# Transposes in pairs of 64-row tiles, output blocks split between ScalarE and GpSimd, and a new instruction order in a fused attention and feed-forward kernel

## Chip, cores and metric

The kernel runs on one core of a Trainium2 chip. The metric is the device time of one execution in microseconds, lower is better. Engines are named as in the profile: PE (TensorE), DVE (VectorE), ACT (ScalarE), POOL (GpSimd), SP (SyncE, which only issues DMAs here).

## What is computed

```python
B, N, m, C = (4, 12480, 32, 128)
scale = 1.0 / np.sqrt(C)
I = np.broadcast_to(inducing[None], (B, m, C))
def mab(q, kv):
    s = scale * (q @ kv.transpose(0, 2, 1))
    s = s - s.max(-1, keepdims=True)
    a = np.exp(s)
    a /= a.sum(-1, keepdims=True) + 1e-09
    return a @ kv
h = mab(I, x)                       # 32 inducing points attend to 12480 rows
attn = mab(x, h)                    # 12480 rows attend to the 32 results
# then, row by row, with w_in [128, 2048] and w_out [2048, 128]
hid = attn @ w_in
out = (hid * np.clip(hid + 3.0, 0.0, 6.0) / 6.0) @ w_out
```

The feed-forward is hid * (hid + 3) / 6 as long as hid lies between -3 and 3: a linear part and a part in products of hid with itself. Since each attention row is a weighted mean of only 32 vectors, the kernel works out the feed-forward of those 32 once per batch (the linear part) and of their pairs (the products), and then gives each row a weighted sum of these coefficients. No 2048-wide hidden layer is ever made for the rows.

## The kernel before

**Tiles.** Each batch of 12480 rows is cut into six groups of 2048 rows (16 tiles of 128 rows) and one small group of 192 rows. Everything is indexed by batch b and group g; g = 6 is the small one.

**Order.** The program is one long list, ORDER (lines 20 to 149), of tokens such as `T.1.2.8.16.6`. Each token calls a function `op_<name>` with the numbers as arguments, and each of these issues a few instructions on one engine. Every engine, and each DMA queue, runs its own instructions in the order of the list and waits where a tile that it needs isn't ready. Letters at a token's end (V, A, P) choose DVE, ACT or POOL. The last number or numbers are banks of PSUM; there are eight banks.

**First attention**, per group: X loads x as 16 bit (POOL's queue, seven buffers xh for the whole groups); T transposes it on PE, eight tiles of 128x128 into one bank; Y copies the bank to xT; S multiplies with the inducing points; E takes the exponential (ACT); A sums x with those weights on PE; H adds that to hacc (DVE).

**Coefficients**, per batch, when all H are done: c3 to cB norm the 32 vectors; G multiplies them with w_in in three parts (a high and a low half of w_in, made by wh and wl at the start); cG writes the result to GL; cD makes two 16-bit copies in Gd. The linear part: cH adds 3 and clips at 0 into r6 (POOL, line 543), cI clips at 6 and multiplies by GL (DVE, line 548), L multiplies with w_out, and cL, cM, cm, cN carry it on. The products: p makes four tiles PR of products of pairs (line 609, 128x2048 each), P multiplies them with w_out on PE (line 616, wb makes the 16-bit w_out), and cP, cX, cY write the result to Cq. cJ takes the largest magnitude of GL for a test at the end; cQ and cC do likewise for other bounds.

**Second attention and output**, per group: Z makes the scores on PE (32-column tiles), Zd, Zz and Ze scale and exponentiate them, W copies some of them to more partitions by DMA (SP's queue, line 698), ee squares (line 692), B spreads the scores on PE in tiles of 32 rows (line 731), F takes the exponential from PSUM to TF (ACT, line 741), U multiplies TF with d into TD (DVE, line 750). Then l (line 770, pairs of 64-row tiles) and q (line 789) build output blocks of 128x512 in a bank: four blocks a group, each of one l and four q for the two factors TF and TD. R, Rr and R2 make the scale r of each row; v multiplies a block by r into os: DVE in one instruction (line 807), ACT in four of 128x128 (line 811). O writes a group's os to DRAM (SP's queue). There are two buffers os, so a group's v wait for the O of two groups earlier.

**Ahead and behind.** w are warming matmuls on zeros. i0 to i9 make constants. y0 to y5 count, at the very end, whether all bounds hold; if one doesn't, the kernel runs `direct_path`, a slow plain version.

Of the kernel before, what the change touches and what calls it, by code (L numbers as in the profile page):

```python
# [9 lines left out]
FP32 = mybir.dt.float32  # L10
# [15 lines left out]
T.0.4.8.16.4 Y.0.4.8.16.4.V S.0.2.0.16.5 E.0.2.0.16.5 H.0.0.0.8.6 X.0.6.0.2 A.0.3.0.16.2 wh.0.A wl.0.V A.0.2.0.16.5
S.0.4.8.16.6 S.0.4.0.8.1 wi.1 T.0.5.8.16.4 T.0.6.0.2.3 T.0.5.0.8.0 E.0.4.0.8.1 Y.0.6.0.2.3.V S.0.6.0.2.7 Y.0.5.0.8.0.V
A.0.4.0.8.3 H.0.3.0.16.2 H.0.4.0.8.3 Y.0.5.8.16.4.A X.1.1.0.16 S.0.5.8.16.4 wh.2.V E.0.6.0.2.7 S.0.5.0.8.1 wh.3.V
E.0.5.8.16.4 X.1.0.0.16 wo.1 A.0.6.0.2.0 H.0.6.0.2.0 A.0.5.8.16.4 wo.0 E.0.4.8.16.6 A.0.4.8.16.7 H.0.5.8.16.4
E.0.5.0.8.1 H.0.4.8.16.7 H.0.2.0.16.5 A.0.5.0.8.6 H.0.5.0.8.6 c3.0.0 wl.3.V T.1.1.0.8.5 c7.0.V wl.1.P c8.0.V  # L30
T.1.1.8.16.4 i7.P G.0.1.2 wl.2.P G.0.3.2 G.0.2.2 Y.1.1.8.16.4.A c4.0.0 c9.0 cB.0.P G.0.0.2 cK.0 Z.0.2.1.7 Zd.0.2.7 cA.0
Z.0.0.0.1 Y.1.1.0.8.5.V cG.0.2 Z.0.0.1.5 Zd.0.0.5 W.0.0.0 W.0.0.2 Z.0.1.1.3 Zz.0.0.1 Z.0.1.0.2 Zd.0.1.3 Zz.0.1.2 W.0.0.1
cD.0.0.V T.1.0.8.16.0 T.1.0.0.8.4 X.1.3.0.16 cH.0.P cD.0.1.A Y.1.0.8.16.0.V S.1.1.0.16.6 Y.1.0.0.8.4.A W.0.0.3
E.1.1.0.16.6 Z.0.3.0.5 Z.0.2.0.7 cI.0 Zz.0.2.7 p.0.2.V W.0.2.3 B.0.0.0.2.0 S.1.0.0.16.4 F.0.0.0.0.2 E.1.0.0.16.4 L.0.0.6
A.1.1.0.16.7 W.0.2.0 H.1.1.0.16.7 L.0.1.6 cL.0.6 p.0.1.V A.1.0.0.16.4 cM.0.0.6 W.0.1.0 Ze.0.0 cm.0.3 ee.0.0.V cN.0.3
# [120 lines left out]
TG = 16  # L156
# [27 lines left out]
def kernel(  # L184
# [35 lines left out]
    with ExitStack() as es:  # L220
# [78 lines left out]
        def veng(e):  # L299
            return {"V": nc.vector, "P": nc.gpsimd}[e]  # L300
# [241 lines left out]
        def op_cH(b, e):  # L542
            veng(e).tensor_scalar(
                r6[:, :, :], GL[:, :, :M].bitcast(FP32), 3.0, 0.0, op0=ALU.add, op1=ALU.max
            )
# [485 lines left out]
```

## Time and profile before

| what | us |
|---|---|
| median of 3 runs | 248.84 |
| lowest and highest run | 248.77 and 250.02 |
| the profiled execution | 249.51 |
| its span, first to last instruction | 247.5 |

The profile describes one execution. Busy time of an engine is the time in which one of its instructions ran; matmuls overlap in their pipeline, so PE's busy time is not its peak rate. A row of the timeline has the start, the time from first start to last end, engine, line, operation, output and inputs, and how many instructions were merged; in brackets the idle time of the engine ahead of it and what ended it. A row of a group has busy time, mean ns of one, and the idle time ahead of them with its releasers. A row of waits has the total, how often, and the longest.

### The profile page before, as it was taken

To read this page: it belongs to the slowest core of one execution; us is meant where nothing else is said; L and a number is where in the kernel's file an instruction comes from. 1 tells how busy PE (TensorE), PEld (TensorE's weight loads), DVE (VectorE), ACT (ScalarE), POOL (GpSimd) and SP (SyncE) were. 2 spreads that over 40 slices of the span, in tenths; PEclk is the share of its full clock that TensorE was granted. 3 is DMA by queue.
4 is the path that set the end of the run, shared out by engine and by line. 5 is a ranking of instruction groups with operands and counts; after the bars stand their busy time and mean duration, and the time that the engine had idled before them with its cause. 6 is when DMAs were issued, how large, how long until landed. Compare 5 with 4: busy or idle time off the path is not lost. (4 is left out here: it accounts for less than half of the span.)

```text
span 247.5 us, 10076 instructions
## 1 busy us (share of the span) xinstructions
PE 227.0 (92%) x4317; PEld 186.5 (75%) x4317; DVE 202.4 (82%) x438; ACT 191.1 (77%) x350; POOL 40.3 (16%) x80
## 2 busy tenths in 40 slices
PE   1879799999799999999899999999999999989990
PEld 0568758888698798797787888888878877768780
DVE  0236879989599997999778998988889999998983
ACT  2167277998788886999687786999889889989870
POOL 8518582021002500010004000000031000000000
PEclk9999679999999999999999999999999999999998
DMA  6999789969989999849879974623981849696953
GB/s 96 193 255 254 238 158 193 208 163 250 214 286 263 277 196 331 293 87 250 184 252 265 266 274 110 224 56 76 338 305 37 262 97 340 211 311 170 362 232 134
DMA packets 23744, 53.91 MB, mean 218 GB/s; under 512 B 3697, under 2 KB 16785, under 8 KB 20753
## 3 DMA queue, kind: packets, MB, share of 16 engines
q1 hardware_dynamic: 19072, 38.36, 47.4%
q0 software_dynamic: 4624, 14.88, 31.0%
q8 instruction: 34, 0.56, 0.8%
q14 instruction: 14, 0.11, 0.1%
HBM read 27.67 MB, written 25.56 MB: 215 GB/s over the span
## 5 line engine op out<-in xcount | busy, mean ns | idle before, releaser
L741 ACT ACTIVATE TF<-ps 128x1024 f16<-128x1024 f32 (+1 forms) x100 | 96.8, 1007 | 16.1 <-PE ps L731 12.4
L750 DVE TENSOR_TENSOR TD<-TF,d 128x2048 f16<-128x2048 f16 (+1 forms) x52 | 59.9, 1156 | 3.0 <-ACT TF L741 2.2
L789 PE MATMUL ps<-Cq,TF 128*128 128x128 f16 (+1 forms) x784 | 57.9, 219 | 2.6 <-issue 1.4
L789 PE MATMUL ps<-Cq,TD 128*128 128x128 f16 (+1 forms) x784 | 56.0, 219 | 0.0
L807 DVE TENSOR_TENSOR os<-ps,r 128x512 f32<-128x512 f32 x68 | 45.4, 683 | 11.7 <-PE ps L789 4.1
L789 PEld LDWEIGHTS <-TF 128*128 128x128 f16 (+1 forms) x784 | 46.3, 98 | 6.3 <-issue 6.0
L789 PEld LDWEIGHTS <-TD 128*128 128x128 f16 (+1 forms) x784 | 46.1, 99 | 4.3 <-issue 3.4
L811 ACT ACTIVATE os<-ps,r 128x128 f32<-128x128 f32 x112 | 32.0, 380 | 4.3 <-PE ps L789 2.0
L422 PE MATMUL ps<-ident_h,xh 128*128 128x128 f16 x384 | 29.8, 226 | 5.5 <-DMA xh<-in_x_dram 5.5
L422 PEld LDWEIGHTS <-xh 128*128 128x128 f16 x384 | 24.0, 102 | 11.6 <-DMA xh<-in_x_dram 7.5
L428 DVE COPY xT<-ps 128x1024 f16<-128x1024 f16 x31 | 21.2, 684 | 12.8 <-PE ps L422 12.5
L428 ACT COPY xT<-ps 128x1024 f16<-128x1024 f16 x17 | 17.0, 1015 | 18.9 <-PE ps L422 18.8
L416 POOL DMA_DIRECT2D xh<-in_x_dram x25 | 13.9, 560 | 75.1 <-PE ps L459 62.2
L731 PE MATMUL ps<-z,pair 32*128 32x256 f16 (+1 forms) x400 | 20.3, 270 | 0.0
L609 DVE TENSOR_TENSOR PR<-Gd 128x2048 bf16<-128x2048 bf16 x16 | 19.8, 1239 | 0.0
L678 DVE TENSOR_SCALAR_CACHE_REDUCE z<-ps 128x512 f16<-128x512 f32 (+1 forms) x28 | 17.3, 621 | 2.4 <-PE ps L656 2.3
L666 ACT ACTIVATE dk<-ps 128x512 f16<-128x512 f32 (+1 forms) x28 | 14.8, 547 | 5.5 <-PE ps L656 3.4
L770 PE MATMUL ps<-BD,ee 64*128 64x256 f16 (+1 forms) x196 | 17.5, 273 | 0.2
L441 ACT ACTIVATE a<-ps 128x512 f16<-128x512 f32 (+1 forms) x27 | 14.6, 556 | 2.6 <-PE ps L433 2.6
L616 PE MATMUL ps<-w_ob,PR 128*128 128x128 bf16 x256 | 16.5, 219 | 0.0
L671 ACT ACTIVATE e<-z 128x512 f16<-128x512 f16 (+1 forms) x28 | 16.3, 589 | 0.1
L616 PEld LDWEIGHTS <-PR 128*128 128x128 bf16 x256 | 14.7, 98 | 0.9 <-issue 0.8
(137 smaller groups left out, 284.8 us busy)
## 6 DMA issues: line engine op xcount, KB each, us to landing
out_dram<-os SPq DMA_DIRECT2D x23, 1024.0 KB, 5.2
d<-dk SPq DMA_DIRECT2D x96, 128.0 KB, 3.9
xh<-in_x_dram POOLq DMA_DIRECT2D x23, 512.0 KB, 8.8
os<-in_moe_w_in_dram POOLq DMA_DIRECT2D x2, 512.0 KB, 13.4
w_or<-in_moe_w_out_dram POOLq DMA_DIRECT2D x2, 512.0 KB, 11.6
out_dram<-os SPq DMA_DIRECT2D x2, 512.0 KB, 3.6
xh<-in_x_dram POOLq DMA_DIRECT2D x2, 256.0 KB, 7.3
out_dram<-osl SPq DMA_DIRECT2D x4, 96.0 KB, 3.0
```

Source lines behind the costliest of these rows:

```text
L422: nc.tensor.transpose(pt[:, (i - lo) * p : (i - lo + 1) * p], at(xh, xhl, b, g)[:p, i, :], ident_h[:p, :p])
L428: copier(e)(xT_of(b, g)[:, lo * p : hi * p], ps[:, k, :].bitcast(FP16)[:, : (hi - lo) * p])
L609: veng(e).tensor_mul(pr_of(b, c)[:, :, :].rearrange("p a (i m) -> p a i m", m=M), views[0], views[1])
L616: nc.tensor.matmul(ps[:, k, f * C : (f + 1) * C], lhsT=pr_of(b, c)[:, jb, :], rhs=w_ob[:, jb, :], start=first_of(b, u), stop=False, skip_g ...
L678: nc.vector.tensor_scalar(fat(z_, b, g)[:rows, :w], ps[:rows, k, :w], 1.0, None, op0=ALU.mult, op1=ALU.min, accum_out=z_all[:rows, b * NGR ...
L731: nc.tensor.matmul(ps[:, pairs[j // 2] + j % 2, f * w : (f + 1) * w], lhsT=pair[rows, f, :], rhs=fat(z_, b, g)[rows, h * w : (h + 1) * w], ...
L741: nc.scalar.activation(hat(TF_, b, g, h)[:, 2 * q : 2 * q + 2, :w], ps[:, k : k + 2, :w], ACT.Exp, scale=scale / KH)
L750: nc.vector.tensor_mul(split(hat(TD_, b, g, h)), split(hat(TF_, b, g, h)), d.unsqueeze(2).to_broadcast([P, J, 2, w]),)
L770: nc.tensor.matmul(ps[:p, ks[jp], s2 * 2 * C : (s2 + 1) * 2 * C], lhsT=fat(e2_, b, g)[rows, s * p : (s + 1) * p], rhs=BD_[b % 2][rows, :, ...
L789: nc.tensor.matmul(ps[:p, k, (s2 * 2 + j2) * C : (s2 * 2 + j2 + 1) * C], lhsT=t[:, j, f * w + s2 * p : f * w + (s2 + 1) * p], rhs=Cq_[b % ...
L807: nc.vector.tensor_mul(o, src, r.unsqueeze(3).to_broadcast([p, Sh, 2, C]))
L811: nc.scalar.mul(o[:, s2, j2, :], src[:, s2, j2, :], r[:, s2, j2 : j2 + 1])
```

## The change

Four things change beside the order of the list.

1. Transposes of the whole groups of batches 1 to 3 (18 groups): TT moves a tile of 128 rows as two transposes of 64 rows, one on the upper and one on the lower half of the array, into two banks; one TT is a whole group, 32 matmuls of 64 columns in place of 16 of 128. YY copies each of the two banks to xT with a stride, 128x1024 as Y does. Batch 0 and the small groups keep T and Y.
2. 13 of 100 output blocks are copied unscaled by ACT in one instruction (`v...C`) and then multiplied in place by POOL (`m`). The others: 64 on DVE (70 before) and 23 on ACT with scaling (30 before).
3. The clip is gone: cI multiplies GL + 3 by GL straight from GL, cH and r6 are removed. The test at the end takes the sum of the squares of GL along each partition (ACT) with a bound of 9, in place of the largest magnitude (DVE) with a bound of 3.
4. Engines: 14 of 28 ee and 4 of 16 p run on POOL, some copies swap between DVE and ACT.

In the list, batch 0's loads come ahead of w_in (w_in's first half stood before its last groups), three groups of batch 1 come ahead of w_out, there are 26 warming matmuls in place of 16, and of the last group R, R2 and the counts y0, y1, y2 stand earlier.

```diff
+        def op_TT(b, g, *ks):
+            for i in range(TG):
+                for r in range(2):
+                    rows = slice(64 * r, 64 * r + 64)
+                    nc.tensor.transpose(
+                        ps[:, ks[r], :].bitcast(FP16)[:, i * 64 : (i + 1) * 64],
+                        at(xh, xhl, b, g)[rows, i, :],
+                        ident_h[rows, rows],
+                        tile_position=(64 * r, 0),
+                    )
+
+        def op_YY(b, g, r, k, e):
+            copier(e)(
+                xT_of(b, g)[:, :].rearrange("c (i r t) -> c r i t", r=2, t=64)[:, r],
+                ps[:, k, :].bitcast(FP16).rearrange("c (i t) -> c i t", t=64),
+            )
...
-        def op_cH(b, e):
-            veng(e).tensor_scalar(
-                r6[:, :, :], GL[:, :, :M].bitcast(FP32), 3.0, 0.0, op0=ALU.add, op1=ALU.max
-            )
-
         def op_cI(b):
             nc.vector.scalar_tensor_tensor(
-                GL[:, :, M:], r6[:, :, :], 6.0, GL[:, :, :M].bitcast(FP32), op0=ALU.min, op1=ALU.mult
+                GL[:, :, M:],
+                GL[:, :, :M].bitcast(FP32),
+                3.0,
+                GL[:, :, :M].bitcast(FP32),
+                op0=ALU.add,
+                op1=ALU.mult,
             )
 
         def op_cJ(b):
-            nc.vector.tensor_reduce(
-                g_all[:, b : b + 1],
+            nc.scalar.activation(
+                junk[:, :].rearrange("p (a m) -> p a m", m=M),
                 GL[:, :, :M].bitcast(FP32),
-                axis=AX.XY,
-                op=ALU.max,
-                apply_absolute_value=True,
+                ACT.Square,
+                accum_out=g_all[:, b : b + 1],
             )
...
-            if e == "V":
+            if e == "C":
+                nc.scalar.copy(o, src)
+            elif e == "V":
                 nc.vector.tensor_mul(o, src, r.unsqueeze(3).to_broadcast([p, Sh, 2, C]))
...
+        def op_m(b, g, h, jp):
+            t0, p, J, Sn = groups[g]
+            Sh = (Sn + 1) // 2
+            o = at(os_, osl, b, g)[:p, : J * Sn, :].rearrange("p (s j) c -> p s j c", j=J)
+            o = o[:, h * Sh : (h + 1) * Sh, 2 * jp : 2 * jp + 2, :]
+            r = r2_of(b, g, 0, J * Sn).rearrange("p (s j) -> p s j", j=J)
+            r = r[:, h * Sh : (h + 1) * Sh, 2 * jp : 2 * jp + 2]
+            nc.gpsimd.tensor_mul(o, o, r.unsqueeze(3).to_broadcast([p, Sh, 2, C]))
...
-            count(3, g_all[:, :], 3.0, ALU.is_le)
+            count(3, g_all[:, :], 9.0, ALU.is_le)
```

The new list around the coefficients of batch 0 and the first q, as it stands (TT and YY carry batch, group and banks or half):

```diff
+E.0.4.0.8.6 X.1.3.0.16 X.1.0.0.16 A.0.5.0.8.4 wo.0 A.0.4.0.8.5 w.2.6 wh.3.V wl.3.V E.0.4.8.16.7 wo.1 E.0.5.8.16.0
+A.0.5.8.16.3 wh.0.A H.0.6.0.2.2 X.1.6.0.2 H.0.5.0.8.4 H.0.4.0.8.5 A.0.4.8.16.1 H.0.5.8.16.3 X.1.2.0.16 TT.1.1.3.2
...
+E.1.0.0.16.7 H.1.1.0.16.0 Ze.0.1 wb.1.P Zz.0.0.1 B.0.0.0.4.0 F.0.0.0.0.4 W.0.1.0 Zz.0.2.6 p.0.1.V L.0.1.3 A.1.0.0.16.2
...
+p.0.3.V Z.0.3.0.7 P.0.0.6 R2.0.1.V cP.0.0.6 Zz.0.3.7 X.1.4.0.16 P.0.3.2 TT.1.5.4.0 TT.1.2.7.1 cN.0.3 Ze.0.2 ee.0.2.V
```

More of the change, by code (lines that the diff above doesn't have):

```diff
@@ L26 @@
[L26 to L35, printed above, removed]
@@ L151 @@
[L151 to L152 removed]
+i2 w.2.5 w.2.0 X.0.0.0.16 i1 i8 w.2.2 w.2.0 w.2.4 i0 w.2.5 i4.1 i3.V w.2.4 i5.1.V X.0.6.0.2 T.0.6.0.2.7 Y.0.6.0.2.7.A
+w.2.1 X.0.1.0.16 T.0.0.8.16.4 Y.0.0.8.16.4.V T.0.0.0.8.6 Y.0.0.0.8.6.V X.0.2.0.16 S.0.0.8.16.0 E.0.0.8.16.0 S.0.0.0.8.2
+i6 A.0.0.8.16.5 E.0.0.0.8.2 A.0.0.0.8.3 w.2.7 T.0.1.0.8.2 Y.0.1.0.8.2.V T.0.1.8.16.6 X.0.3.0.16 w.2.4 S.0.6.0.2.1
@@ new lines @@
+l.0.1.1.5.7 ee.0.4.V v.0.1.1.0.5.A ee.0.3.P Z.0.5.1.6 Zd.0.5.6 q.0.2.0.1.1.4 q.0.2.0.1.0.4 B.0.3.0.2.0 F.0.3.0.1.0
+v.0.1.1.1.7.V l.0.2.0.5.4 TT.2.4.6.7 q.0.2.0.0.1.5 S.1.4.0.16.0 F.0.3.0.0.2 X.3.0.0.16 U.0.2.1 E.1.4.0.16.0
+q.0.2.0.0.0.5 R2.0.2.V O.0.0.0.16 v.0.2.0.1.4.C YY.2.4.0.6.V Z.0.5.0.2 m.0.2.0.1 YY.2.4.1.7.V B.0.3.1.6.0 F.0.3.1.0.6
+X.2.3.0.16 q.0.2.1.0.1.3 v.0.2.0.0.5.V W.0.3.2 W.0.3.1 Zz.0.5.2 R.0.4.4 Rr.0.4.4 U.0.3.0 q.0.2.1.1.1.5 F.0.3.1.1.0
+W.0.4.2 q.0.2.1.1.0.5 q.0.2.1.0.0.3 l.0.2.1.3.5 W.0.4.3 B.0.4.0.6.0 v.0.2.1.1.5.V A.1.4.0.16.2 H.1.4.0.16.2
@@ new lines @@
+q.1.3.1.0.0.7 cJ.1 cC.2 Rr.1.6.6 q.1.3.0.0.0.4 v.1.3.0.0.4.V B.1.4.1.0.2 F.1.4.1.1.2 l.1.3.1.7.6 ee.1.6.V G.2.2.5
+G.2.3.5 F.1.4.1.0.0 cG.2.5 cI.2 q.1.3.1.1.0.6 cD.2.1.A q.1.3.1.1.1.6 B.1.5.0.2.4 F.1.5.0.0.2 cA.2 S.3.1.0.16.1 cD.2.0.V
+L.2.0.0 U.1.4.0 q.1.3.1.0.1.7 v.1.3.1.1.6.A W.1.5.2 p.2.2.V q.1.4.1.1.0.3 ee.1.4.P v.1.3.1.0.7.A L.2.1.0 cL.2.0
+E.3.1.0.16.1 q.1.4.1.0.0.6 q.1.4.0.0.0.2 q.1.4.0.0.1.2 U.1.4.1 p.2.3.P l.1.4.1.6.3 l.1.4.0.2.1 W.1.6.0 F.1.5.0.1.4
+TT.3.4.7.0 YY.3.4.0.7.V W.1.5.3 O.1.2.0.16 v.1.4.0.0.2.A TT.3.2.4.5 YY.3.2.1.5.V YY.3.2.0.4.A q.1.4.1.1.1.3
@@ new lines @@
+l.2.0.0.3.1 H.3.3.0.16.7 O.1.4.0.16 v.1.6.0.0.2.V B.2.1.0.4.6 q.2.0.0.0.0.3 Ze.2.3 F.2.1.0.0.4 R.2.2.0 q.2.0.0.0.1.3
+q.2.0.0.1.1.1 ee.2.1.V U.2.0.1 F.2.1.0.1.6 S.3.5.0.16.2 Rr.2.2.0 q.2.0.1.1.0.4 v.2.0.0.0.3.A R2.2.1.V W.2.1.2
+A.3.4.0.16.5 E.3.5.0.16.2 q.2.0.0.1.0.1 W.2.1.1 W.2.1.3 U.2.1.0 H.3.4.0.16.5 v.2.0.0.1.1.V Z.2.4.0.0 Z.2.4.1.5 Zd.2.4.5
+B.2.1.1.6.2 dr Zz.2.4.0 A.3.5.0.16.1 q.2.0.1.1.1.4 H.3.5.0.16.1 F.2.1.1.0.6 W.2.2.3 c3.3.1 R.2.3.0 Rr.2.3.0
+q.2.0.1.0.0.5 c4.3.1 q.2.0.1.0.1.5 F.2.1.1.1.2 U.2.1.1 R2.2.2.V l.2.0.1.5.4 v.2.0.1.0.5.C m.2.0.1.0 B.2.2.0.0.6
@@ L153 @@
+q.3.5.1.0.0.4 Ze.3.6 q.3.5.1.0.1.4 F.3.6.0.0.0 U.3.6.0 v.3.5.0.1.6.A ee.3.6.V v.3.5.0.0.5.V q.3.6.0.0.0.2 v.3.5.1.0.4.V
+R.3.6.1 Rr.3.6.1 R2.3.6.V l.3.6.0.2 m.3.4.1.0 O.1.6.0.2 O.3.4.0.16 O.3.5.0.8 y1 v.3.5.1.1.7.A q.3.6.0.0.1.2 O.3.5.8.16
+y3 y4.3 y5.3 v.3.6.0.0.2.A O.3.6.0.2
 """
@@ L258 @@
         Gd = sb.tile([P, FB, 2 * M], BF16, name="Gd")
-        r6 = sb.tile([P, FB, M], FP32, name="r6")
         LV = sb.tile([2 * M, C], FP32R, name="LV")
```

228 lines of the change are left out of this document (106 added, 122 removed).

## The prediction

> **What bounds the kernel now.** I read the page first (share of each engine, the 40 slices), then the busy time in three stretches, then the waits of the longest stretch.
>
> ```profile
> span 247.5 us, 10076 instructions
> PE 227.0 (92%) x4317; PEld 186.5 (75%) x4317; DVE 202.4 (82%) x438; ACT 191.1 (77%) x350; POOL 40.3 (16%) x80
> PE   1879799999799999999899999999999999989990
> PEclk9999679999999999999999999999999999999998
> DMA  6999789969989999849879974623981849696953
> ```
>
> The reader is to see TensorE near nine tenths in nearly every slice but the first seven and the last, a clock that drops in slices 5 to 7, and DMA engines near full over that same start.
>
> ```profile
> 0.00:47.40 47.40, 37.46 (x690) 29.43 (x691) 27.60 (x66) 25.84 (x40) 24.70 (x58) 0.93 0.93 200
> 47.40:241.00 193.60, 189.17 (x3625) 156.91 (x3623) 172.54 (x352) 164.62 (x309) 15.56 (x22) 1.00 0.77 224
> 241.00:247.50 6.50, 0.39 (x7) 0.14 (x5) 2.29 (x22) 0.62 (x2) 0.00 (x0) 0.84 0.40 149
> 27.00:33.90 6.90, 6.24 (x91) 4.56 (x92) 4.91 (x16) 2.77 (x5) 3.19 (x4) 0.51 0.82 205
> 47.38 1.05 PE L789 MATMUL ps<-Cq,TF 128*128 128x128 f16 x16
> ACT TF L741 <- PE ps L731: 11.3, 22, 1.7
> DVE os L807 <- DMA out_dram<-os: 3.5, 3, 1.7
> ```
>
> The columns are stretch, length, busy time of PE, PEld, DVE, ACT and POOL, clock, DMA share, GB/s. I cut at 47.4 because the first q (line 789) starts at 47.38. From there to 241 TensorE is idle for 193.60 - 189.17 = 4.4 us, DVE is busy 89% and ACT 85%, and the largest wait has ACT waiting for TensorE. So this stretch is **TensorE's instruction stream**: time taken from it comes off the span while DVE and ACT hold. The start is set by loads (DMA share 0.93) and by the first batch's chain of coefficients, part of it at half clock (0.51 in the fourth row).
>
> **The transposes.** Now 16 matmuls of 128 columns move a group; after, 32 of 64 columns do, in pairs on two halves of the array. 18 groups change, batch 0 and the small groups don't.
>
> ```profile
> 19.45 1.05 PE L422 MATMUL ps<-ident_h,xh 128*128 128x128 f16 x16
> L422 PE MATMUL ps<-ident_h,xh x384: 216/219/314, 6.5 to 173.0; 128*128 128x128 f16 x192
> 19.05 0.55 PE L433 MATMUL ps<-I_T,xT 128*128 128x32 f16 x16
> L433 PE MATMUL ps<-I_T,xT 128*128 128x32 f16 x384 | 13.3, 177 | 0.0
> 236.11 0.44 PE L789 MATMUL ps<-Cq,TD 128*128 128x128 f16 x5
> 236.49 0.61 PE L770 MATMUL ps<-BD,ee 64*128 64x256 f16 x8
> L770 PE MATMUL ps<-BD,ee 64*128 64x256 f16 x192 | 16.9, 272 | 0.2
> 237.03 0.26 PE L731 MATMUL ps<-z,pair 32*128 32x96 f16 x4
> L731 PE MATMUL ps<-z,pair 32*128 32x96 f16 x16 | 1.0, 206 | 0.0
> ```
>
> A run of n matmuls lasts n-1 distances plus one duration. Old transposes: (1.05 - 0.219) / 15 = 55 ns each, 0.89 us a group. The shortest distance on the whole array is that of S: (0.55 - 0.177) / 15 = 25 ns. Now tiles: the eight matmuls of l (64 rows, 256 columns) have their starts within 0.61 - 0.27 = 0.34 us; four pairs in turn make three distances of 113 ns, so the two of a pair run side by side (in series at twice 55 ns per 128 columns it would be 0.77 us). Pairs of B with 96 columns: 0.26 - 0.206 = 54 ns. Between these, (113 - 54) / 160 = 0.37 ns a column, and 64 columns come to 42 ns a pair; half of the old 55 gives 28 ns. I take 35 ns, between the two: 16 x 35 = 0.56 us, **0.33 us less a group**. Bounds: 28 ns a pair (0.44 us less) and 2 x 25 = 50 ns with no overlap (0.09 us less). Changing the tile layout costs too: the last of the five q starts at 236.11 + 0.44 - 0.22 = 236.33, l at 236.49: 0.16 us where 0.055 is usual, so 0.1 us a change. I counted the changes of layout along both lists: 178 before, 180 after, since most TT stand beside l or B; 0.2 us in all.
>
> The Trainium skill's page "TensorEngine Tiling (Array Packing)", section "Instruction Overhead", speaks against the edit: a matmul carries some 60 cycles, and no tiling factor is to be taken from a dimension that is already small. The row of S agrees that there is a floor on one tile; the row of l shows that two tiles share the time. By that rule the price is the 50 ns of the rival below.
>
> **The start.** Each X moves a whole group; T waits for it.
>
> ```profile
> 9.62 0.76 PE L422 MATMUL ps<-ident_h,xh 128*128 128x128 f16 x8 [0.36 <-DMA xh<-in_x_dram]
> 13.29 0.62 PE L422 MATMUL ps<-ident_h,xh 128*128 128x128 f16 x8 [0.87 <-DMA xh<-in_x_dram]
> 27.66 0.63 PE L481 MATMUL ps<-I,hacc 128*128 128x32 f32 x2 [1.50 <-DVE hacc L476]
> 31.32 0.69 DVE L532 TENSOR_TENSOR GL<-ps,rD 128x512 fp32r<-128x512 f32 x1 [0.84 <-PE ps L523]
> 32.11 1.93 POOL L543 TENSOR_SCALAR r<-GL 128x512 f32<-128x512 f32 x1 [1.80 <-DVE GL L532]
> ```
>
> Between the two T waits one group and a half landed: 3.67 / 1.5 = 2.45 us a group, the pace of the start. Before, w_in's first half stands ahead of the last groups of x; after, all of batch 0 comes first. With the first at 6.5, the last lands near 6.5 + 0.3 + 5 x 2.45 = 19, w_in (two pieces of half a group's bytes) near 22. ACT then queues wh.2 ahead of three E: E, A and H end near 25, wl.0 near 27, G and cG near 28 instead of 31.3. The clip's 1.93 us on POOL leaves the chain cG, cI, L; what is late next is w_out: it now comes after three groups of batch 1, near 22 + 3 x 2.45 + 2.5 = 32, and L waits for it in TensorE's order, with S and B behind it. The first q stands behind TT.1.5, whose X comes two groups and a small one later, near 37.3; about ten W share the queues (a group's time, say 2 us), then TT, cX, cY: q near 41.5 to 42, against 47.38. TensorE has by then done about the same work, one group's TT more. I take **5 us**; bounds 0 (it waits for loads instead) and 7. Ten more warming matmuls lie in waits for loads.
>
> **DVE, ACT and GpSimd.**
>
> ```profile
> L807 DVE TENSOR_TENSOR os<-ps,r 128x512 f32<-128x512 f32 x68 | 45.4, 683 | 11.7 <-PE ps L789 4.1 <-DMA out_dram<-os 3.5 <-ACT TF L741 2.9
> L811 ACT ACTIVATE os<-ps,r 128x128 f32<-128x128 f32 x112 | 32.0, 380 | 4.3 <-PE ps L789 2.0 <-PE ps L770 1.1 <-ACT e L671 1.0
> L609 DVE TENSOR_TENSOR PR<-Gd 128x2048 bf16<-128x2048 bf16 x16 | 19.8, 1239 | 0.0
> L692 DVE TENSOR_TENSOR ee<-e 128x512 f16<-128x512 f16 x24 | 9.8, 413 | 0.3 <-PE ps L770 0.3
> L553 DVE TENSOR_REDUCE g_all<-GL 128x1 f32<-128x512 f32 x4 | 2.7, 665 | 0.0
> L641 ACT ACTIVATE junk<-Cp 128x512 f32<-128x512 f16 x4 | 2.5, 635 | 0.0
> L666 ACT ACTIVATE dk<-ps 128x512 f16<-128x512 f32 x24 | 14.1, 598 | 4.2 <-PE ps L656 3.4 <-ACT TF L741 0.6
> L405 POOL TENSOR_TENSOR w_lo<-os,w_hi 128x512 bf16<-128x512 f32 x2 | 3.1, 1536 | 0.8 <-DVE w_hi L402 0.7
> L543 POOL TENSOR_SCALAR r<-GL 128x512 f32<-128x512 f32 x4 | 8.6, 2143 | 7.1 <-DVE GL L532 4.1 <-DVE r L723 2.8 <-DVE hm L506 0.3
> 81.64 1.61 DVE L750 TENSOR_TENSOR TD<-TF,d 128x2048 f16<-128x2048 f16 x1
> L750 DVE TENSOR_TENSOR TD<-TF,d 128x2048 f16<-128x2048 f16 x48 | 58.7, 1224 | 2.8 <-ACT TF L741 2.0 <-DMA d<-dk 0.8
> ```
>
> DVE gives up 6 v (4.1), 14 ee (5.8), 4 p (5.0), the cJ (2.7) and some copies: about 18 us. ACT does 13 plain copies at 0.60 (as line 666), 7.8; 7 fewer scaled blocks at a merged 4 x 32.0 / 112 = 1.14, -8.0; four cJ at some 0.83, 3.3; two cD, one wh and one Y, 3.3: about 6 us more. GpSimd gets 27 products of 512 elements (m, ee), at the 1.54 of line 405, 42 us, and 4 of 2048 at four times that, 6.2, 25 us, and loses 8.6 of the clip. No row has these forms: the bounds are 0.41 (ee on DVE) and 2.75 (the longest clip, 1.43 times its usual 1.92) for a small one, 1.24 and 11 for a large one. POOL stays under half busy; X issues queue behind these products, but X waited 62.2 us in all for free buffers, so they have slack. A product on POOL also slowed a U beside it: 1.61 us at 81.64 against a mean of 1.22. At a quarter of 52 U that is 5 us of DVE, less than it gave up.
>
> With 4.3 us off TensorE (13 groups x 0.33 behind the first q), ACT would stand at (164.6 + 6) / 189.3 = 90%, so some of its waits return. I take **1.5 us of new waits**, bounds -2 (DVE's relief ends waits) and 8.
>
> **The end.** R, R2 and most counts of the last group move ahead of the last q; y3 remains. I take 0.5 us, bounds 0 and 1.
>
> **Sum.** From the profiled execution, 249.5 us (span 247.5 and 2.0 around it): -5.0 -4.3 +0.2 +1.5 -0.5 = -8.1, 241.4. The median shown, 248.84, lies 0.7 below that execution; so 240.7.
>
> **Rivals.**
> - **Pairs in series.** TensorE's floor of 25 ns holds over both tiles: 13 x (0.33 - 0.09) = 3.1 us back, 243.8. For it: no row has pairs under 54 ns. Against: the rows of l.
> - **The start gains nothing**, since w_out, TT.1.5 and the loads bind: 5 us back, 245.7. For it: DMA share 0.93, and L now stands early in TensorE's order. Against: the last of batch 0 comes some 3 us sooner.
> - **GpSimd holds TensorE (slower).** In batch 1, P.1.1 follows p.1.1 on POOL by five short blocks of TensorE (two cM, two Z, B: some 2 us). TensorE waits there for what the product lasts beyond its lead, at four places. At 6.2 us with leads of 2 to 9 us the loss is about 4 us; at 9 to 11 us with DVE beside it (the 1.43 times above), ee and m queue behind as well and each large product costs 2 to 5 us more: 10 to 12 us lost, 251.5. It decides from some 2.5 us lost per product and as much on output buffers (two only, with O now behind m).
>
> The Trainium skill's "GPSIMD Engine Reference", section "Key points", says that GpSimd shares its SBUF interfaces with VectorE and contends with instructions that have two SBUF inputs; the U of 1.61 us agrees.
>
> **How the numbers follow.** My forecast has 0.62 (236.5 to 243.5), pairs in series 0.12, no gain at the start 0.12, GpSimd 0.10, and 0.04 for several losses that cancel the gain. Half a per cent, 1.2 us, is what a measurement tells from no change. Faster 0.86, same 0.04, slower 0.10. The range reaches from the forecast's low bounds (28 ns pairs, 7 us at the start, no new wait: 235) over both faster rivals to 247.5.
>
> **What would show it.** L789's first start near 42; TT rows with starts 28 to 42 ns a pair; no clock of 0.5 between 27 and 34; cI right behind cG; TensorE's idle time behind the first q near 6 us; POOL's products at 1.5 and 6 us. Wrong would be: PE waiting for PR written by POOL, TT rows of 1.0 us for 32, L or TT long idle for DMA.

## The result and the profile after

| | before | after |
|---|---|---|
| median, us | 249.43 (248.77 to 254.33, 4 runs) | 270.56 (265.56 to 272.66, 4 runs) |
| profiled execution, us | 249.51 | 272.66 |
| its span, us | 247.5 | 270.9 |

The changed kernel is slower: the ratio is 1.0735, with a 95% interval of 1.0535 to 1.0936. The forecast was 240.7, and even the slower rival, 251.5, lies far below. Some executions run in a slower state at a lower granted clock: the ratio leaves these out and sets 265.56 and 269.50 against 248.77, 248.84 and 250.02, and the profiled execution of the changed kernel (granted clock 0.93) is one of them, so its gaps are at the large side.

The page of the changed kernel, its span, its busy times and three rows of slices:

```profile
span 270.9 us, 10725 instructions
PE 233.2 (86%) x4615; PEld 190.3 (70%) x4615; DVE 210.1 (78%) x408; ACT 197.1 (73%) x350; POOL 82.3 (30%) x104
PE   7876987698996867999996859999999999999770
PEclk9999798999999587999998866999999999999987
DMA  6999979769999743987699003755895758397671
```

A slice is 6.8 us. TensorE has holes in slices 13 to 16 (81 to 108 us) and 22 to 24 (142 to 163 us), and the clock is low there too. DVE was to lose some 13 us of busy time and has 7.7 more (210.1 against 202.4). The same kernel's busy times by stretch, cut at its first q and at its last (columns as in the prediction: stretch, length, PE, PEld, DVE, ACT, POOL, clock, DMA share, GB/s), and two shorter stretches:

```profile
0.00:49.30 49.30, 39.46 (x808) 30.47 (x809) 31.27 (x66) 28.12 (x44) 23.52 (x60) 0.93 0.95 205
49.30:262.10 212.80, 193.37 (x3807) 159.67 (x3805) 176.55 (x325) 168.35 (x305) 58.76 (x44) 0.94 0.69 203
262.10:270.90 8.80, 0.40 (x7) 0.14 (x5) 2.29 (x21) 0.62 (x2) 0.00 (x0) 0.77 0.22 81
89.40:96.20 6.80, 6.23 (x107) 6.08 (x105) 4.17 (x10) 3.94 (x9) 0.42 (x2) 0.50 0.56 200
157.60:167.80 10.20, 7.94 (x86) 6.61 (x86) 7.74 (x11) 2.34 (x6) 3.10 (x2) 0.50 0.07 16
```

The span grew by 23.4 us: 1.9 in the start (49.3 against 47.4), 19.2 in the middle (212.8 against 193.6) and 2.3 at the end (8.8 against 6.5). In the middle TensorE idles 19.4 us where it idled 4.4, and it is busy 4.2 us longer though its transposes are shorter; parts of the stretch run at half clock, as the last two rows show. Added up over the windows of the clock records that begin between 10 us and 12 us before the end, the changed kernel has 34.1 us at half clock, the kernel before 6.8.

What TensorE waited for in that stretch, the five largest rows (total, times, longest):

```profile
PE ps L803 <- DVE TD L764: 3.9, 2, 3.4
PE ps L432 <- DVE z L692: 3.8, 1, 3.8
PE ps L745 <- DVE rc L731: 2.4, 1, 2.4
PE ps L784 <- ACT dk L680: 2.2, 1, 2.2
PE ps L432 <- DVE LV L586: 1.3, 1, 1.3
```

Four of the five are VectorE, the engine that the change was to relieve, and none is a PR written by GpSimd, which was my sign of the slower rival. The groups say which of VectorE's instructions grew, and what GpSimd's products last (busy time, mean ns of one, idle time before):

```profile
L764 DVE TENSOR_TENSOR TD<-TF,d 128x2048 f16<-128x2048 f16 (+1 forms) x52 | 70.5, 1359 | 5.3 <-DMA d<-dk 3.2
L623 DVE TENSOR_TENSOR PR<-Gd 128x2048 bf16<-128x2048 bf16 x12 | 20.8, 1748 | 0.0
L623 POOL TENSOR_TENSOR PR<-Gd 128x2048 bf16<-128x2048 bf16 x4 | 16.9, 4236 | 14.9 <-DVE Gd L555 12.3
L836 POOL TENSOR_TENSOR os<-os,r 128x512 f32<-128x512 f32 x13 | 18.8, 1443 | 103.5 <-ACT os L821 93.3
L706 POOL TENSOR_TENSOR ee<-e 128x512 f16<-128x512 f16 x14 | 17.5, 1249 | 16.9 <-ACT e L685 12.2
```

GpSimd is as fast as I had reckoned or faster (4.24 us a large product, 1.25 and 1.44 a small one; I took 6.2 and 1.54), although these means contain time in which it stood still beside VectorE: the shortest are 3.67 and 1.03. But a p left on VectorE takes 1748 ns in place of 1239, and the 52 U take 70.5 us in place of 59.9. The timeline shows where that time sits (start, length, engine, line, operation, count, idle time before):

```profile
96.51 3.81 POOL L623 TENSOR_TENSOR PR<-Gd 128x2048 bf16<-128x2048 bf16 x1
100.26 1.04 POOL L706 TENSOR_TENSOR ee<-e 128x512 f16<-128x512 f16 x1
96.80 5.60 DVE L764 TENSOR_TENSOR TD<-TF,d 128x2048 f16<-128x2048 f16 x1
98.38 0.64 PE L432 MATMUL ps<-ident_h,xh 64*128 64x64 f16 x32
103.06 1.03 PE L432 MATMUL ps<-ident_h,xh 64*128 64x64 f16 x32 [3.82 <-DVE z L692]
149.28 9.44 POOL L623 TENSOR_TENSOR PR<-Gd 128x2048 bf16<-128x2048 bf16 x2 [12.28 <-DVE Gd L555]
150.19 4.89 DVE L623 TENSOR_TENSOR PR<-Gd 128x2048 bf16<-128x2048 bf16 x1
155.25 4.54 DVE L764 TENSOR_TENSOR TD<-TF,d 128x2048 f16<-128x2048 f16 x1
159.86 2.74 PE L803 MATMUL ps<-Cq,TD 128*128 128x128 f16 x24 [3.39 <-DVE TD L764]
```

The U at 96.80 starts 0.3 us after GpSimd's product and ends at 102.40, 1.1 us after GpSimd's next product, an ee, which ends at 100.26 + 1.04 = 101.30: 5.60 us for work of 1.22. It looks as if it stood still for as long as GpSimd computed. VectorE's z stands behind it, a transposition waits for z's bank, and TensorE idles 3.8 us. At 150 us it happens twice in a row. Behind the gaps the clock is halved: the same 32 transposes take 0.64 us at 98.38 and 1.03 us at 103.06.

### The profile page after: what moved, and what is told of

It is laid out like the page before. It is cut to its first block, busy times and chain, and to the rows that moved or that the text cites. A ratio compares the mean times of both kernels' runs of the same rounds, so it can differ in the third digit from the quotient of the medians.

```text
span 270.9 us, 10725 instructions
## 1 busy us (share of the span) xinstructions
PE 233.2 (86%) x4615; PEld 190.3 (70%) x4615; DVE 210.1 (78%) x408; ACT 197.1 (73%) x350; POOL 82.3 (30%) x104
## 4 chain that ended last, share of the span: by engine, by line
PE 51%; DMA 18%; DVE 13%; ACT 6%; SPq 4%; issue 3%; POOL 1%; DVEq 0%; ACTq 0%; POOLq 0%
PE ps L803 24%; DMA out_dram<-os 11%; DVE TD L764 5%; PE ps L745 4%; SPq L712 4%; DMA d<-dk 4%; PE ps L630 4%; PE ps L784 4%; DMA xh<-in_x_dram 4%; PE ps L670 3%; ACT TF L755 3%; PE ps L432 2%; PE ps L464 2%; PE ps L448 2%; DVE PR L623 2%
## 5 line engine op out<-in xcount | busy, mean ns | idle before, releaser
L755 ACT ACTIVATE TF<-ps 128x1024 f16<-128x1024 f32 (+1 forms) x100 | 96.0, 1006 | 13.8 <-PE ps L745 13.2
L764 DVE TENSOR_TENSOR TD<-TF,d 128x2048 f16<-128x2048 f16 (+1 forms) x52 | 70.5, 1359 | 5.3 <-DMA d<-dk 3.2
L803 PE MATMUL ps<-Cq,TD 128*128 128x128 f16 (+1 forms) x784 | 60.5, 227 | 3.9 <-DVE TD L764 3.9
L823 DVE TENSOR_TENSOR os<-ps,r 128x512 f32<-128x512 f32 x61 | 40.7, 682 | 17.1 <-DMA out_dram<-os 7.9
L836 POOL TENSOR_TENSOR os<-os,r 128x512 f32<-128x512 f32 x13 | 18.8, 1443 | 103.5 <-ACT os L821 93.3
L827 ACT ACTIVATE os<-ps,r 128x128 f32<-128x128 f32 x88 | 25.3, 379 | 7.5 <-PE ps L803 6.7
L440 ACT COPY xT<-ps 128x1024 f16<-128x1024 f16 x13 | 13.1, 1018 | 15.3 <-PE ps L432 15.3
L706 POOL TENSOR_TENSOR ee<-e 128x512 f16<-128x512 f16 x14 | 17.5, 1249 | 16.9 <-ACT e L685 12.2
L623 POOL TENSOR_TENSOR PR<-Gd 128x2048 bf16<-128x2048 bf16 x4 | 16.9, 4236 | 14.9 <-DVE Gd L555 12.3
L432 PE MATMUL ps<-ident_h,xh 64*128 64x64 f16 x576 | 13.1, 201 | 9.5 <-DVE z L692 3.8
L623 DVE TENSOR_TENSOR PR<-Gd 128x2048 bf16<-128x2048 bf16 x12 | 20.8, 1748 | 0.0
L432 PEld LDWEIGHTS <-xh 64*128 64x128 f16 x576 | 11.3, 102 | 12.4 <-issue 11.0
```

Of the source, the lines that this page charges most:

```text
L432: nc.tensor.transpose(ps[:, ks[r], :].bitcast(FP16)[:, i * 64 : (i + 1) * 64], at(xh, xhl, b, g)[rows, i, :], ident_h[rows, rows], tile_po ...
L623: veng(e).tensor_mul(pr_of(b, c)[:, :, :].rearrange("p a (i m) -> p a i m", m=M), views[0], views[1])
L706: veng(e).tensor_mul(fat(e2_, b, g)[:rows, :w], e_in, e_in)
L755: nc.scalar.activation(hat(TF_, b, g, h)[:, 2 * q : 2 * q + 2, :w], ps[:, k : k + 2, :w], ACT.Exp, scale=scale / KH)
L764: nc.vector.tensor_mul(split(hat(TD_, b, g, h)), split(hat(TF_, b, g, h)), d.unsqueeze(2).to_broadcast([P, J, 2, w]),)
L803: nc.tensor.matmul(ps[:p, k, (s2 * 2 + j2) * C : (s2 * 2 + j2 + 1) * C], lhsT=t[:, j, f * w + s2 * p : f * w + (s2 + 1) * p], rhs=Cq_[b % ...
```

## The experiments

Theories: **exclusion** (a GpSimd product and a VectorE instruction with both operands in SBUF don't run side by side; the longer one sets the pace), **order** (the new list itself is worse), **pairs** (the 64-row transposes starve the clock). A fourth, **gate**, came out of misses: a task on GpSimd decides when the loads of x behind it in GpSimd's queue go out, and loads that go out earlier delay other transfers.

The kernel before ran beside each set of experiments. Its medians were 250.78 beside e1 to e4, 250.99 beside e5 to e8, 250.09 beside e9 to e12 and 249.43 beside e13 to e16, with single runs from 246.3 to 254.6. A median below is over 4 runs where nothing is said, and a ratio stands with its 95% interval.

### The four products

**e1**, the changed kernel with them back on VectorE:

```diff
-p.1.0.P ... p.1.1.P ... p.2.3.P ... p.2.1.P
+p.1.0.V ... p.1.1.V ... p.2.3.V ... p.2.1.V
```

> The changed kernel with its four large products p on DVE again. Theory (lock): a GpSimd product and a DVE instruction with two SBUF inputs run one after the other, whichever came first; the four large ones (4.2 us mean) hold U and p, DVE's queue stops, TensorE idles and its clock halves. It expects 250 us (245 to 257), no U over 2.5 us, and the half clock gone from 89 to 106 and from 147 to 168. Rival (order): the new list itself is at fault, through loads and W; expects 265 or more. Rival (pairs): 64-row transposes starve the clock; expects 265 or more, the clock halved at the same places.

Measured: 257.13 (251.12 to 260.34), 13 us below the changed kernel and at the upper end of what exclusion gave. No U lasts over 2.2 us and the half clock is gone from both places, as expected; behind the first q, 10.2 us of it are left, at 83 and 168 us. **e6** does the reverse to the kernel before, where nothing else is new:

```diff
-p.1.0.V ... p.1.1.V ... p.2.3.V ... p.2.1.V
+p.1.0.P ... p.1.1.P ... p.2.3.P ... p.2.1.P
```

> The kernel before, with nothing changed but the engine of the same four products (p.1.0, p.1.1, p.2.1, p.2.3: GpSimd instead of VectorE). If GpSimd's product and VectorE's two-input product shut each other out wherever they meet (lock), this alone costs the kernel before much of the 13 us that e1 won back: 256 to 264, with products of 3 us or more on GpSimd, U of 3 to 5.6 us beside them, and new half-clock windows behind the gaps. If the damage needs the new order, 249 to 252.

Measured: 262.38, ratio 1.0493 (1.0385 to 1.0601), so 11.4 us lost by four tokens, as exclusion gave. No load is at fault: the rows of waits put all but 1 us of TensorE's named waits (13.8 us in all with 2.7 of issue, 4.2 in the kernel before) on VectorE. The timeline of e6 shows which instructions are held:

```profile
85.11 8.96 POOL L611 TENSOR_TENSOR PR<-Gd 128x2048 bf16<-128x2048 bf16 x2 [3.10 <-DVE Gd L542]
86.87 3.55 DVE L550 SCALAR_TENSOR_TENSOR GL<-r,GL 128x512 fp32r<-128x512 f32 x1
90.35 0.68 DVE L809 TENSOR_TENSOR os<-ps,r 128x512 f32<-128x512 f32 x1
90.95 3.16 DVE L725 TENSOR_TENSOR r<-rc 128x16 f32<-128x16 f32 x1
144.02 4.15 POOL L611 TENSOR_TENSOR PR<-Gd 128x2048 bf16<-128x2048 bf16 x1
144.44 4.01 DVE L694 TENSOR_TENSOR ee<-e 128x512 f16<-128x512 f16 x1
```

The two products run from 85.11 to 85.11 + 8.96 = 94.07. A v, with one operand in PSUM (line 809), keeps its usual 0.68 us in the middle of that. A product of 16 columns with both operands in SBUF (line 725), 0.17 us elsewhere, takes 3.16 and ends when GpSimd ends; the ee at 144.44, usually 0.42, takes 4.01. A VectorE reduction with one operand, in SBUF, keeps its 0.17 us at 141.01 inside a GpSimd product (139.15 to 143.44). In these rows the exclusion does not depend on the VectorE instruction's size, but on how many of its operands are in SBUF, and on which engine came first.

**e12** is e6 with the four products on GpSimd made one-operand passes, so the product is left out of the coefficients:

```diff
-            veng(e).tensor_mul(pr, views[0], views[1])
+            if e == "P":
+                nc.gpsimd.tensor_scalar(pr, views[1], 0.25, 0.0, op0=ALU.add, op1=ALU.max)
+            else:
+                nc.vector.tensor_mul(pr, views[0], views[1])
```

> e6 (the kernel before with four products on GpSimd) with those four made one-operand passes of the same shape on GpSimd: the pass adds a constant to one of the two views and writes PR, so the product is left out. If the exclusion needs two operands in SBUF on both engines, VectorE's two-operand instructions beside these passes keep their 1.2 us (U), the passes take 2 to 5 us, and the time falls from 262.4 to 249 to 254. If any long GpSimd instruction does it, it stays at 259 to 264.

Measured: 268.37, ratio 1.0841 (1.0725 to 1.0956): a miss. The time tells nothing of the condition, since these passes take 7 to 8 us where the products took 4.2, and hold up the loads queued behind them (TensorE waits 4.9 us for an xh). The rows tell more:

```profile
141.68 7.59 POOL L613 TENSOR_SCALAR PR<-Gd 128x2048 bf16<-128x2048 bf16 x1
143.85 3.92 DVE L754 TENSOR_TENSOR TD<-TF,d 128x2048 f16<-128x2048 f16 x1
147.69 0.41 DVE L696 TENSOR_TENSOR ee<-e 128x512 f16<-128x512 f16 x1
148.31 0.68 DVE L550 SCALAR_TENSOR_TENSOR GL<-r,GL 128x512 fp32r<-128x512 f32 x1
```

The U is still held, but it ends 1.5 us before the pass does, and ee and cI run at their usual pace beside it. So a one-operand pass shuts VectorE out for part of its time only. Which part stays open. That the pass is so long could have been read from the kernel before: its clip, a pass with the same two steps over 512 elements, takes 1.92 us, and four times that, an estimate, is 7.7.

### ee, m, and the loads behind them

**e2** puts the 14 ee back on VectorE (`ee.*.P` to `ee.*.V`), **e3** takes the 13 m off GpSimd (`v...C` and its `m` become one `v...A`), **e4** does e1, e2 and e3 together, so that GpSimd has none of these products left.

> The changed kernel with the 14 ee of GpSimd on DVE again, p and m kept there. Lock: ee hold back the p of DVE at 39 to 45 us (2.05 and 2.83 us instead of 1.24) and some U, some 8 us of DVE in all, but the four large products stay: 262 us (257 to 267), first q 3 us earlier. Order and pairs: 267 or more.

> The changed kernel with the 13 plain copies scaled by ACT again and no product m on GpSimd. Lock: m cost DVE only some 3 us (U of 1.3 to 2.1 us), and ACT gets 7 us more: 266 us (262 to 271). If m and the two output buffers set the pace instead, it falls to 255 or less.

> The changed kernel with no product on GpSimd (p and ee on DVE, the 13 blocks scaled by ACT): the pairs of 64-row tiles, no clip and the new list remain. Lock: what is left is the forecast without GpSimd, 243 us (238 to 249), clock at full speed behind 45 us. Order: 255 or more. Pairs: 255 or more, with the clock halved behind TT.

Measured: e2 273.17, ratio 1.0970 (1.0814 to 1.1126); e3 277.11, ratio 1.1161 (1.1041 to 1.1280); e4 264.78, ratio 1.0624 (1.0522 to 1.0727). All three missed: neither ee nor m off GpSimd brings anything (why e3 is even slower than the changed kernel was not tried), and e4, with no exclusion by a product left, is slower than e1. Its trace shows one large hole, in the rows of waits of TensorE and ScalarE between 47 and 58 us:

```profile
PE ps L784 <- ACT dk L680: 8.6, 1, 8.6
ACT dk L680 <- DMA d<-dk: 9.0, 1, 9.0
```

and in its timeline, GpSimd and TensorE:

```profile
38.77 0.53 POOL L414 DMA_DIRECT2D xh<-in_x_dram  x1 [3.30 <-PE ps L718]
39.55 1.05 POOL L414 DMA_DIRECT2D xh<-in_x_dram  x2 [0.25 <-issue]
57.38 0.61 PE L784 MATMUL ps<-BD,ee 64*128 64x256 f16 x4 [8.64 <-ACT dk L680]
```

The three loads X.2.1, X.1.4 and X.2.2 go out at 38.8 to 40.1 us, since nothing on GpSimd stands ahead of them any more. Of the first batch's W transfers, four that follow land at 53.1 to 56.8 us by the DMA records, 12 to 14 us after their issue. ScalarE can't reuse a dk, TensorE waits for ScalarE, and 10.2 us from 52.7 us on run at half clock. The changed kernel waits 2.2 us at the same place, e2 5.9 us. **e7** changes one token of e4:

```diff
-ee.0.0.V
+ee.0.0.P
```

> The kernel of e4 with one token changed: ee.0.0 on GpSimd again, ahead of the loads X.2.1, X.1.4 and X.2.2 in GpSimd's queue. In e4 these three go out at 38.8 to 40.1 us, four of the first batch's W transfers land behind them (53.1 to 56.8 us), and TensorE waits 8.9 us; in e1 they go out at 41.1 to 42.2 us and no W is late. If that wait and the half clock behind it (10.2 us from 52.7 us) are what keeps e4 slow (loads ahead of W), one instruction that holds the loads back brings 8 to 12 us: 253 to 257 from 264.8. If not, 263 to 266.

Measured: 254.98, as the gate theory gave, ratio 1.0224 (1.0118 to 1.0329): 9.8 us by one ee moved back to GpSimd. Its timeline:

```profile
41.59 1.45 POOL L706 TENSOR_TENSOR ee<-e 128x512 f16<-128x512 f16 x1 [6.28 <-ACT e L685]
42.99 1.66 POOL L414 DMA_DIRECT2D xh<-in_x_dram  x3
```

The ee waits for ScalarE and so holds the loads to 43.0 us; seven W are ahead of them now, and the wait is gone. **e16** does the same to e2:

> e2 (the changed kernel with the 14 ee back on VectorE; 273.2) with one of them, ee.0.0, left on GpSimd ahead of the loads X.2.1, X.1.4 and X.2.2. In e2 these go out at 39.1 to 40.5 us and TensorE waits 6.1 us for the W transfers behind them (2.5 us in the changed kernel). Theory gate: e2's miss is this wait, and the time falls to 263 to 268. Rival (ee on GpSimd costs nothing, its place neither): 271 to 275.

Measured: 268.52, ratio 1.0751 (1.0669 to 1.0834), 4.7 us below e2 and half a us above what the gate theory gave. The wait of 5.9 us is gone from its rows. So this wait is part of e2's miss, not all of it: e16, with 13 of the 14 ee back on VectorE, is no faster than the changed kernel (ratio 1.0735). The rows of e2 show where the rest may have gone, and e16 has the same at the same place (TensorE's wait is 5.60 us there):

```profile
149.76 9.42 POOL L624 TENSOR_TENSOR PR<-Gd 128x2048 bf16<-128x2048 bf16 x2 [12.48 <-DVE Gd L556]
155.47 4.00 DVE L707 TENSOR_TENSOR ee<-e 128x512 f16<-128x512 f16 x1
159.52 1.03 PE L785 MATMUL ps<-BD,ee 64*128 64x256 f16 x8 [6.86 <-DVE ee L707]
```

An ee put back on VectorE is itself an instruction with both operands in SBUF. Here it stands still beside the large products that were left on GpSimd, and TensorE waits for it.

### The clip

**e8** was meant to keep the good parts alone: the kernel before, eleven groups in pairs at the place of their second bank, and no clip.

```diff
-T.1.3.8.16.2 ... Y.1.3.8.16.2.A ... T.1.3.0.8.1 ... Y.1.3.0.8.1.A
+TT.1.3.3.1 ... YY.1.3.0.3.A YY.1.3.1.1.A
...
-cH.0.P
```

> The kernel before with two parts of the change and none of the others: eleven groups of batches 1 to 3 transposed as pairs of 64-row tiles at the place of their second bank, and no clip (the GpSimd pass over r6 is gone, the maximum is a sum of squares on ScalarE). All on the engines and in the order of before. By the rows of the traces: a group's 32 matmuls 0.64 to 0.71 us against 16 of 55 ns (0.88 us), so 11 x 0.2 = 2.2 us, and some 1 us of the first batch's coefficient chain: 245.5 to 248.5 against 249. If the pairs starve the clock or their copies cost: 251 or more.

Measured: 256.15 (6 runs), ratio 1.0230 (1.0150 to 1.0310), slower. Two kernels take it apart: **e9** has only the clip gone, **e11** is e8 with 128-row transposes at e8's places.

> The kernel before with the clip alone taken out (no pass over r6 on GpSimd, the maximum on VectorE becomes a sum of squares on ScalarE); same engines, order and transposes. If the clip's pass is on the path of each batch's coefficients, 246.5 to 249; if the list has slack there, no difference from 250.8 (undisturbed 247 to 251). If e8's loss came with this part (ScalarE's 0.6 us passes between its exponentials), 252 or more.

> e8 with its eleven pairs turned back into 128-row transposes at the same moved places (both halves of a group together, at the place of the second); no clip as in e8. If e8's loss (256 against 251) is of the moving, this is as slow as e8 or 1 to 3 us slower: 255 to 259. If it is of the pairs, 249 to 252.

Measured: e9 255.48 (6 runs), ratio 1.0315 (1.0228 to 1.0402); e11 258.53 (6 runs), ratio 1.0345 (1.0218 to 1.0472). Taking an instruction of 2 us off GpSimd alone costs as much as e8 lost, and the moved transposes add nothing that these runs can tell. It need not be the same loss: the wait of e9 shown below is not in the traces of e8 and e11, where TensorE waits for nothing longer than 1.6 us behind the first q, so where these two lose their time stays open. ScalarE's sum of squares, which I had named, is not it, since e13 below keeps it. The timeline of e9 on four engines:

```profile
127.45 1.10 POOL L417 DMA_DIRECT2D xh<-in_x_dram  x2
128.40 0.59 SPq L845 DMA_DIRECT2D out_dram<-os  x1
142.38 1.14 ACT L830 ACTIVATE os<-ps,r 128x128 f32<-128x128 f32 x4 [5.76 <-DMA out_dram<-os]
143.58 1.07 PE L748 MATMUL ps<-z,pair 32*128 32x256 f16 x7 [4.14 <-ACT os L830]
```

and of the kernel before at that place:

```profile
131.24 1.92 POOL L543 TENSOR_SCALAR r<-GL 128x512 f32<-128x512 f32 x1 [2.76 <-DVE r L723]
133.12 1.15 POOL L416 DMA_DIRECT2D xh<-in_x_dram  x2
```

Before, the clip waits for VectorE and holds two loads to 133.1 us. Without it they go out at 127.5, ahead of the store of an output group; that store lands at 142.28 us by the DMA records, instead of 135.48, ScalarE waits 5.8 us for the buffer os, and B on TensorE 4.1 us for ScalarE. **e13** puts another small task in the clip's place:

```diff
-cD.2.0.A
+cD.2.0.P
```

> e9 (the kernel before without the clip, 255.5) with one token changed: the half copy cD.2.0 runs on GpSimd instead of ScalarE, ahead of the loads X.3.2 and X.3.5 in GpSimd's queue, where the clip's pass stood. In e9 these loads go out at 127.5 and 128.0 us (133.1 and 133.7 in the kernel before), the output store issued at 128.4 us lands at 142.3 us (135.5), ScalarE waits 5.8 us for that buffer and TensorE 4.4 us for ScalarE. Theory gate (a task on GpSimd times the loads behind it): the wait goes, 249 to 251.5. Rival (the loss is in ScalarE's sum of squares or the coefficients): 254 to 256.

Measured: 251.16 (12 runs), ratio 1.0043 (0.9994 to 1.0092). Its GpSimd, on the timeline:

```profile
133.32 0.61 POOL L558 CAST Gd<-GL 128x512 bf16<-128x512 f32 x1 [2.66 <-DVE GL L550]
133.87 1.10 POOL L417 DMA_DIRECT2D xh<-in_x_dram  x2
```

The loss is gone, with the rest of e9 as it was. The gate is shown twice, on different transfers and in different orders. The moved token also frees its old engine, but by 0.4 us of VectorE in e7 and 0.6 us of ScalarE here, against 9.8 and 4.3 us won.

### The pairs

**e5** is e1, and **e15** is e7, with 128-row transposes in place of all pairs (each TT becomes two T into the same banks, each YY a Y). **e10** has pairs in the kernel before, only in the four groups whose two banks were already held together.

> The kernel of e1 (the four products p back on VectorE) with every pair of 64-row transposes turned back into two banks of 128-row transposes at the same place of the list. The profile of e1 has 31.2 us... of TensorE time less what it needs elsewhere: transposes of both forms take 20.0 us from start to start there, 25.3 us in the kernel before. If the pairs give what they are worth by themselves, taking them out costs 2 to 5 us: 259 to 262 against 257 (251 undisturbed: 253 to 256). If the pairs are what holds the clock down (the rival), the half-clock windows (17 us in e1) go below 10 us and the time falls to 250 or less.

> e7 (new order, nothing of p, ee and m on GpSimd but ee.0.0; 255.0) with 128-row transposes in place of every pair. If the pairs are worth their TensorE time in this order (transposes of both forms 20.5 us from start to start in e7 against 25 to 27), 257 to 260. If they are worth nothing where other engines set the pace, 253 to 256. If they hurt, 252 or less.

> The kernel before with four groups (1.0, 1.1, 1.2, 2.2) transposed as pairs of 64-row tiles where both banks were already held together, nothing moved by more than four places. By the rows: 4 x 0.2 = 0.8 us less TensorE time: 248 to 250.5. If the pairs themselves hurt (the clock, the strided copies), 252 or more.

Measured: e5 254.01 (250.12 to 262.40) against e1's 257.13 (251.12 to 260.34), too spread to tell. (The profile of e5 has 6.8 us at half clock and that of e1 17.1, as the theory of starving gave, but the two profiled executions, 253.34 and 260.34, lie 7 us apart, less than either kernel's runs among themselves.) e15 254.26 (6 runs), ratio 1.0176 (1.0105 to 1.0246), against e7's 1.0224: no difference. e10 249.64 (12 runs), ratio 1.0050 (0.9994 to 1.0106): none either. The pairs neither pay nor harm. The theory that they starve the clock finds no support: e7 with them has 17.1 us at half clock, e15 without them 13.7, and they take the same time, and e6, with none, gets its loss with 6.8. What becomes of the saved time can be read in e7 and e15: behind the first q, TensorE is busy 188.1 us with the pairs and 191.9 without, but idle 9.7 and 5.6, in stretches of the same length (197.8 and 197.5).

**e14** is e13 and e10 together:

> e13 with the four groups whose banks are held together (1.0, 1.1, 1.2, 2.2) as pairs of 64-row tiles, as in e10. The start of e9 (first output product at 45.8 us against 47.4) and of e10 (45.2) were both earlier than before's: if they add and nothing is given back, 247.5 to 249.5, against 250.1; if the list takes the gain up again, 249.5 to 251.

Measured: 248.74 (247.16 to 251.76, 12 runs), ratio 0.9954 (0.9915 to 0.9993). It is the only version ahead of the kernel before, by about half a per cent, hardly more than the measurement can tell, and neither of its parts alone shows it (1.0043 and 1.0050).

## Why the prediction was wrong

**GpSimd beside VectorE: the step that failed.** I wrote that a product on GpSimd slows a U beside it from 1.22 to 1.61 us, "at a quarter of 52 U that is 5 us of DVE, less than it gave up". The row that I used was that of the clip, a pass with one operand. With two operands on both engines the rows show exclusion: U of 5.60 and 4.54 us. The term itself, 0.39 us for each meeting, was the mis-sized one: a meeting costs up to the whole length of GpSimd's product. VectorE's busy time, which by my sum was to fall by 13 us, rose by 7.7. The sentence of the Trainium skill that I had cited ("GPSIMD Engine Reference", "Key points": shared interfaces, contention with two SBUF inputs) is borne out, far more strongly than the row that I set beside it; I took the agreement of a weak row for its size. I also looked at the wrong victim: the rival "GpSimd holds TensorE" let TensorE wait for PR, while it waits for z, TD, rc and LV, which are queued on VectorE behind a held instruction. Shown by e1 (13 us) and e6 (11.4 us). My rival had 0.10 and 251.5; the price per product was about right (2.5 us named as the point from which it decides, about 3 measured), the chance was not.

**"X issues queue behind these products, but ... they have slack": failed too.** I asked whether loads could come too late and never whether they could come too early. Of the clip's removal I counted only the chain that it shortens. e9 and e13, e4 and e7 show that the tasks on GpSimd time the loads, at 4 to 10 us a place. In the changed kernel itself the wait of this kind is 2.2 us, so this is a gap in the reasoning more than a large part of its loss.

**The start: failed.** Forecast 41.5 to 42 us for the first q, measured 49.33 (row below). The new start delivers little: cG starts at 30.09 us where I had 28, and P then waits for products that an ee on GpSimd holds up. I had priced the way to the first q by loads alone. The load that I named last, X.1.5, lands at 38.71 by the DMA records (37.3 forecast), but its TT runs only at 46.16, behind P, and P waits for VectorE, whose four products p begin at 36.30 and end at 44.58. The rival "the start gains nothing" was closer. In e2, with no ee on GpSimd, the first q starts at 47.33, just as in the kernel before.

```profile
49.33 0.61 PE L803 MATMUL ps<-Cq,TF 128*128 128x128 f16 x8
30.09 0.68 DVE L547 TENSOR_TENSOR GL<-ps,rD 128x512 fp32r<-128x512 f32 x1
44.63 1.60 PE L630 MATMUL ps<-w_ob,PR 128*128 128x128 bf16 x16 [1.69 <-DVE PR L623]
```

**The clock: missing from the sum.** Most idle gaps of TensorE of over 1 us in the changed kernel were followed by one to three windows of 3.4 us at half clock (not all: none right after those at 14 and 51 us). So a wait may cost more than its length. By how much here was not separated; from the stretches it is an estimate: the middle is busy 4.2 us longer although 13 groups at about 0.41 us should take 5.3 off, some 9.5 us in all. Against that, e6 lost its 11.4 us with 6.8 us at half clock, as much as the kernel before, though 3.4 of it stand behind the first q, where the kernel before has none.

**The transposes: right, even larger than reckoned, and of no worth.** From first start to last end, the 32 matmuls last 0.63 to 0.64 us at full clock, where the 16 of before took 1.05: 0.41 us less a group, where I had 0.33. The starts of the 32 lie within 0.45 us, which is 29 ns a pair against my 35 and just inside my bounds (28 and 50), and the rival "pairs in series" is out. The strided copies cost as much as the plain ones (682 ns against 684). But e10 and e15 show that time off TensorE's instruction stream (by these rows 1.6 us for four groups and 5.3 for thirteen) brings nothing measurable: my first claim, that time taken from it in the middle stretch comes off the span, holds only while the list's other engines and transfers keep their places.

**The end:** 2.3 us longer where I had 0.5 less. No run was made on it. By the rows, VectorE's last computation starts 2.8 us behind the last q in both kernels (264.92 and 243.83), so the counts that moved ahead gained nothing, and the longer part lies behind it.

**What stays open:** e15, the new order with no pairs and a single ee on GpSimd, is still 1.8% slower than the kernel before, with some 4 us of it behind the first q; the runs don't say which of its places holds that. The runs of e1 and e5 spread over 9 and 12 us, so neither has a ratio. And why only some gaps are followed by half clock was not tried.

## What to carry to other kernels

Before moving a product to GpSimd, list VectorE's instructions with both operands in SBUF that may meet it, and price each meeting at the product's whole length, then look at who is queued behind the held one. Before taking work off an engine that also issues loads, look at what it holds back: a task that costs nothing can be what keeps a load out of the way of a more urgent transfer, and a cheap task put in its place tells so at once. In a list tuned to its waits, time saved on the busiest engine can be worth nothing, as here; ask the trace which wait ends last instead.

## What the runs showed of the hardware

- VectorE instructions with both operands in SBUF stood still beside a GpSimd product, whatever their size: 16 columns took 3.16 us (usually 0.17), an ee 4.01 (0.42), a U 5.60 (1.22), while one with an operand in PSUM kept its 0.68. (The U met two GpSimd products in a row, the others one.) The Trainium skill's "GPSIMD Engine Reference", section "Key points", calls this contention; here it is exclusion.
- A GpSimd pass with one operand over 2048 elements in bf16 took 7.1 to 8.2 us, longer than the product of two views (4.2), and held VectorE's U for part of that only.
- Pairs of 64-row transposes on two halves of the array ran at 29 ns a pair (starts 3 and 26 ns apart), a whole one of 128 columns at 55.
- The clock fell to half in windows of 3.4 us or multiples of that, in the changed kernel mostly behind idle gaps of TensorE: 34.1 us there, 6.8 in the kernel before, where gaps of 1.4, 1.1 and 1.1 us (62, 121 and 222 us) were followed by none.
- Transfers of 128 KB issued behind three loads of 512 KB landed 12 to 14 us after their issue (e4); issued ahead of the loads, 2.7 us (the first of e7).
